# Where the weight conversions of a spectral-mixing and MLP kernel stand: behind the sums of batch 0's groups, and their late loads on GpSimd's queue

## The chip, the cores and the metric

The kernel runs on one core of a Trainium2 chip. A core has five engines with instruction queues of their own: TensorE (PE in the profile; its weight loads are the row PEld), VectorE (DVE), ScalarE (ACT), GpSimd (POOL) and SyncE (SP). Each engine works through its queue strictly in order, and waits on semaphores for the others. DMAs are issued from the queues of SP, ACT and POOL and run on 16 DMA engines that the three share. The metric is the device time of one execution in microseconds; a run gives one time, and the numbers compared are medians of several runs.

## The reference

Two blocks follow each other. The first filters each of 8 sequences of 3008 tokens with 256 channels in the frequency domain, the second is an MLP with the activation h - tanh(h):

```python
X = np.fft.rfft(x, axis=1)                       # x: (8, 3008, 256)
Y = X * (filt_r + 1j * filt_i)[None, :, :]
y = np.fft.irfft(Y, n=3008, axis=1).astype(np.float32)

h = y.reshape(24064, 256) @ w_in                 # (256, 2048), float64
g = h - np.tanh(h)
out = (g @ w_out).astype(np.float32)             # (2048, 256), float64
```

The two weight matrices arrive as 64-bit floats and are 512K numbers each.

## The kernel before, in words

**The transform.** 3008 is 64 x 47, so the transform is done in two matrix steps each way: over the 64 (`first`, matrices `f`), over the 47 (`forth`, matrices `mats`), the product with the filter (`filtered`), back over the 47 (`back`, `back0`) and back over the 64 (`last`, matrices `g`, product `pu`). The 32 rows between the two steps are worked in seven groups (`SLOTS`): six of 120 partitions and a last one of 48. Between the steps the data of the other batches pass through DRAM (`ct1`, `ct2`); for batch 0 the first step is turned on the chip instead (`first0` writes `turnt`, which lies in the space of `wd`; `across` transposes it), and only its way back goes through `ct2`.

**The weights.** [...] `converted` (L139) loads a piece of 128 x 512 raw numbers with one DMA (`raw`, L143, 512 KB) and makes 32-bit floats from the bits: one ACT step (L149) and six DVE steps (L151, L154, L157, L160, L162, L169; the pieces of the second matrix take L169 in two halves). It is a Python generator: each `next` issues one step. A quarter of a matrix is two such pieces ("jobs"); quarters 0 to 3 are the first matrix (`wu`), 4 to 7 the second (`wd`). `weights` (L210) strings jobs together and begins the load of a later job whenever one is done (`ahead`); `sums` (L194) then adds four products' worth of weight sums per quarter, which the steps of the second stage with seven products need.

**The order.** Nothing is scheduled by a tool: the order of each queue is the order in which the Python code issues (`tc.manual_schedule`). The code before the second stage (L934 to L1057) is batch 0's opening. It loads x in three pieces (L947 on SP, L952 on POOL), the half matrices `fh` on ACT's queue (L949), and the first three raw jobs on ACT's, SP's and POOL's queue (L945, L966). `warmer(n)` issues n products into a tile nobody reads. `first0(c)` works on the piece c of x; behind it `convert(7)` issues one job's steps. Then the loop over the seven groups (L1023) issues for group g: the filter rows of g+2 and `across(g+2)`, `forth` of g+1, then on DVE the sum and difference of group g (L292, L293, which read the product `pa` from PSUM) and the filter products (L303, L308, L309, L310); the sum L312 goes to POOL for all groups but the last; four conversion steps (L1040); and `back0` of g-1 on PE. In the iteration of group 5 it begins the late raw jobs on SP's queue (L1045) and the first loads of `first(2, ...)`: `f` (L242) and `x_sb` (L224, L230), three buffers each. Behind the loop come the products of batch 1's first piece (`first1`, L993), `back` of group 6 (L334), the load of `e` (L413) for the first `pu` and the rest of the early conversions.

The second stage runs steps U = 0, 1, 2, ...; four make one group of tokens. In step U it issues `up` for U, the activation (`shrink`) for U-1 and `down` for U-2. U < 4 use plain forms (`up_plain`, `down_plain`: two or four products of 448 columns, each PSUM bank copied by ACT or DVE, L542); from U = 4 on seven products replace eight (L469, L639), which need the sums of the weights. Quarter k of `wu` is needed at U = k, quarter k of `wd` at U = k + 2. Inside a step, hooks `d`, `e`, `s` and `t` place pieces of other work between the products: conversions (`converting`), the steps of the transforms of later batches (`steps`, `firsts`, `mids`) and the filter copies (`copies`, whose zero tile L1077 is set by POOL and written by SP, L1079).

```python
def e():
    next(dw, None)
    converting(1 + (U > 3))
```

## Time and profile before

| | |
|---|---|
| median of 3 runs | 2756.82 us (2756.11 to 2758.78) |
| the profiled execution | 2759.41 us, span 2757.4 us |
| mean granted clock of TensorE | 0.994 |
| busy share of the span | PE 98%, PEld 86%, ACT 63%, DVE 61%, POOL 47% |
| chain that ended last | PE 91%, DVE 5% |
| first product of group 0 across (L894) | 31.77 us |
| first product back of group 6 (L334) | 86.98 us |
| first `pu` product (L431) | 98.54 us |

A row of a timeline gives the start, the time, the engine, the line and the instruction with its tiles, the number of instructions merged into it, and in brackets how long the engine stood idle before it and what released it. "PE L872" is a matmul issued by line 872; rows of ACTq, SPq and POOL with DMA_DIRECT2D are DMA issues, not the transfers. A row of a source line gives the least, the median and the longest duration in nanoseconds. The granted clock is the share of full speed that the chip's throttle gave TensorE in a window.

### The profile page before, as it was taken

Reading aid. Unit: us, or ns where it says so; the run is one execution under the profiler, and the core shown is the slowest. Engines: PE = TensorE matmul, PEld = TensorE weight load, DVE = VectorE, ACT = ScalarE, POOL = GpSimd, SP = SyncE. Lnnn points to the kernel's source line nnn. Section 1 sums busy time; section 2 is a strip of 40 time slices with the busy share of each in tenths; the row PEclk is TensorE's granted clock in tenths of the full one; section 3 lists DMA queues with packets and bytes.
Section 4 is the critical chain, followed back from the end, with each engine's and each line's share of the span. In section 5 each row is a group of like instructions: output and inputs, shape, how many; then the busy total and the mean of one; then the engine's idle time right before and its main releaser. Section 6 shows DMA issues by size and latency. Waiting matters only on the chain.

```text
span 2757.4 us, 36442 instructions
## 1 busy us (share of the span) xinstructions
PE 2711.3 (98%) x12938; PEld 2367.4 (86%) x12938; DVE 1676.0 (61%) x2082; ACT 1732.1 (63%) x2595; POOL 1292.4 (47%) x1062
## 2 busy tenths in 40 slices
PE   8899999999999999999999999999999999999998
PEld 7578889888898888988889888898888988899887
DVE  6767766566556665666556665466655766644545
ACT  3466666666666666666666666666666666666665
POOL 3015445544554445544445455455444554455452
PEclk9899999999999999999999999999999999999999
DMA  7653322331233312433224232332322222111010
GB/s 203 212 169 88 85 63 71 88 98 49 64 75 102 89 48 60 106 76 79 53 65 109 66 80 53 94 78 67 84 51 69 53 63 53 30 26 32 22 25 17
DMA packets 337532, 207.77 MB, mean 75 GB/s; under 512 B 226390, under 2 KB 299042, under 8 KB 337085
## 3 DMA queue, kind: packets, MB, share of 16 engines
q1 hardware_dynamic: 296157, 151.08, 22.4%
q10 hardware_dynamic: 39056, 48.25, 5.8%
q0 software_dynamic: 2128, 6.03, 0.8%
q8 instruction: 104, 1.70, 0.3%
q14 instruction: 87, 0.71, 0.1%
HBM read 133.31 MB, written 74.97 MB: 76 GB/s over the span
## 4 chain that ended last, share of the span: by engine, by line
PE 91%; DVE 5%; issue 2%; DMA 1%; ACT 1%; ACTq 0%; SPq 0%; POOL 0%; DVEq 0%; POOLq 0%
PE o L639 38%; PE x L469 22%; PE z L469 11%; PE y L469 5%; PE pa L287 3%; PE pe L334 3%; PE pu L431 3%; PE pf L255 2%; PE o L693 1%; DVE h L591 1%; DVE h L525 1%; DVE h L492 1%; DVE xy L324 0%; PE pf L872 0%; PE o L539 0%
## 5 line engine op out<-in xcount | busy, mean ns | idle before, releaser
L639 PE MATMUL o<-t,wd 128*128 128x256 f32 (+1 forms) x3008 | 760.3, 375 | 0.0
L449 POOL TENSOR_TENSOR t<-h 128x512 f32<-128x512 f32 (+1 forms) x186 | 256.5, 1379 | 974.0 <-DVE h L591 856.9
L591 DVE TENSOR_TENSOR h<-h,y 128x1024 f32<-128x1024 f32 (+1 forms) x384 | 512.5, 1335 | 286.0 <-ACT y L587 285.5
L639 PEld LDWEIGHTS o<-t,wd 128*128 128x128 f32 x3008 | 570.5, 190 | 69.5 <-issue 2.4
L469 PE MATMUL x<-tu,wu 128*128 128x256 f32 (+1 forms) x2256 | 574.2, 377 | 1.3 <-ACT u L475 1.0
L639 PE MATMUL o<-h,wd 128*128 128x256 f32 (+1 forms) x2256 | 571.0, 376 | 1.8 <-DVE h L591 1.8
L469 PEld LDWEIGHTS x<-tu,wu 128*128 128x128 f32 x2256 | 421.7, 190 | 62.1 <-ACT u L475 9.2
L639 PEld LDWEIGHTS o<-h,wd 128*128 128x128 f32 x2256 | 424.2, 190 | 52.7 <-DVE h L591 2.6
L475 ACT COPY s<-x 128x512 f32<-128x512 f32 (+1 forms) x188 | 108.7, 578 | 502.2 <-PE x L469 489.7
L581 ACT ACTIVATE y<-h 128x1024 f32<-128x1024 f32 (+1 forms) x384 | 400.1, 1042 | 13.8 <-ACT a L256 6.4
L584 ACT ACTIVATE y<-y 128x1024 f32<-128x1024 f32 (+1 forms) x384 | 399.1, 1039 | 12.1
L587 ACT ACTIVATE y<-y 128x1024 f32<-128x1024 f32 (+1 forms) x384 | 399.8, 1041 | 5.4 <-ACT a L256 0.8
L509 DVE TENSOR_TENSOR h<-z,u 128x512 f32<-128x512 f32 (+1 forms) x188 | 127.6, 679 | 259.1 <-ACT u L475 258.0
L475 ACT COPY u<-x 128x512 f32<-128x512 f32 (+1 forms) x376 | 215.0, 572 | 86.5 <-PE x L469 64.9
L451 POOL TENSOR_TENSOR t<-h 128x512 f32<-128x512 f32 (+1 forms) x186 | 266.8, 1434 | 0.0
L450 POOL TENSOR_TENSOR t<-h,t 128x512 f32<-128x512 f32 (+1 forms) x186 | 259.8, 1397 | 14.6
L452 POOL TENSOR_TENSOR t<-h,t 128x512 f32<-128x512 f32 (+1 forms) x186 | 263.3, 1416 | 0.0
L517 DVE COPY h<-x 128x512 f32<-128x512 f32 (+1 forms) x188 | 127.9, 680 | 157.3 <-PE x L469 156.7
L469 PE MATMUL z<-ut,wu 128*128 128x256 f32 (+1 forms) x752 | 190.3, 375 | 0.0
L469 PE MATMUL z<-tu,wu 128*128 128x256 f32 (+1 forms) x752 | 190.1, 375 | 0.0
L469 PE MATMUL x<-ut,wu 128*128 128x256 f32 (+1 forms) x752 | 190.1, 375 | 0.0
L469 PE MATMUL y<-ut,wu 128*128 128x256 f32 (+1 forms) x752 | 190.0, 375 | 0.0
(143 smaller groups left out, 3096.2 us busy)
## 6 DMA issues: line engine op xcount, KB each, us to landing
e<-ct SPq DMA_DIRECT2D x48, 512.0 KB
ct<-e ACTq DMA_DIRECT2D x96, 240.0 KB
ct<-a ACTq DMA_DIRECT2D x82, 256.0 KB
a<-ct SPq DMA_DIRECT2D x42, 480.0 KB
ft<-filt SPq DMA_DIRECT2D x42, 480.0 KB
out_dram<-ot SPq DMA_DIRECT2D x1248, 16.0 KB
x_sb<-in_x_dram SPq DMA_DIRECT2D x154, 128.0 KB
gt<-g SPq DMA_DIRECT2D x48, 256.0 KB
```

The costliest lines, as they stand in the source:

```text
L449: by.tensor_sub(t[0], b[0][1], b[0][0])
L450: by.tensor_sub(t[1], b[1][1], t[0])
L451: by.tensor_sub(t[2], b[1][1], b[0][1])
L452: by.tensor_sub(t[3], b[1][0], t[1])
L469: nc.tensor.matmul(bank[:, k], wu[:, q - 1, (2 * u + k) * 128:(2 * u + k + 1) * 128], rhs[q - 1], start=(first and k == 0), stop=True, ski ...
L475: ACT.copy(t, X)
L517: V.tensor_copy(h[:, 2, :, 0:w], X)
L581: ACT.activation(y[k], ht[k], AF.Arctan, scale=TURN)
L584: ACT.activation(y[k], y[k], AF.Tanh, scale=BEND)
L587: ACT.activation(y[k], y[k], AF.Square, scale=SCALE, accum_out=y_sums[:, 2 * U + k // 2:2 * U + k // 2 + 1])
L591: V.tensor_mul(ht[k], ht[k], y[k])
L639: nc.tensor.matmul(product(q), wd[:, q - 1, (2 * u + k) * 128: (2 * u + k + 1) * 128], rhs[q - 1][:, k], start=(u == 0 and k == 0 and q == ...
```

## The change

The change is made in the opening and in the hooks of the second stage; the functions that compute are untouched.

- Quarter 3 of the first matrix leaves the early jobs: `early` converts quarters 0 to 2 (six jobs for eight). The late jobs are quarters 4, 3, 5, 6, 7 in this order, ten for eight, and their sums move back by two jobs.
- Raw job 0 is loaded on ACT's queue behind all three `fh` (the first matrix of the transform), where it stood behind the second.
- The warm-up products: 17, 2 and 3 for 13, 5 and 8 in the opening; 4 new ones ahead of `back` of group 6 and 8 for 10 behind it.
- Four conversion steps are issued behind `across(0)`, ahead of group 0. In groups 1 to 5 three steps stand between the sum and difference (L292, L293) and the filter products, where four stood behind these in groups 0 to 5. Three more follow the loop. The rest of the early jobs comes behind the issue of `e`'s load, and four steps of the late jobs are issued before the second stage's tiles are opened, four in place of sixteen behind that.
- The late raw jobs are issued from POOL's queue in place of SP's.
- In the second stage, `e` issues one step up to U = 2 and three from U = 3 on (one up to U = 3, two from U = 4 on); `t` always issues two (one up to U = 1).

```diff
@@ -931,7 +931,7 @@
             f0 = pro.tile([128, NH, 128], F32, name="f0")
             warm_b = cst.tile([128, 1], F32, name="warm_b")
             V.memset(warm_b, 0.0)
-            jobs = parts_of(range(4))
+            jobs = parts_of(range(3))
             sgn = cst.tile([128, 1], F32, name="sgn")
             for half in range(2):
                 V.memset(sgn[64 * half:64 * half + 64], 1.0 - 2 * half)
@@ -942,8 +942,7 @@
                 xt = big([128, 8, DM], F32, "x0")
                 xs.append(xt)
                 if c == 2:
-                    began += [begun(tiles0, job, queue=q)
-                              for job, q in zip(jobs, (ACT, nc.sync))]
+                    began.append(begun(tiles0, jobs[1], queue=nc.sync))
                 nc.sync.dma_start(xt[0:64], dram(x.tensor, r * DM, [[NR * DM, 64], [1, 8 * DM]]))
                 fh = pro.tile([128, 8, 64], F32, tag="e1", bufs=5, name="fh")
                 ACT.dma_start(fh, half_d[:, 64 * r:64 * r + 512])
@@ -956,6 +955,7 @@
                     n = cols.stop - cols.start
                     V.tensor_scalar(out=f0[:, r:r + 8, to:to + n], in0=fh[:, :, cols],
                                     scalar1=sgn, scalar2=None, op0=ALU.mult)
+            began.insert(0, begun(tiles0, jobs[0], queue=ACT))
             nc.sync.dma_start(one, one_d)
             nc.sync.dma_start(mats[:, 0:3 * KM], mats_d[:, 0:3 * KM])
             ACT.activation(warm_b, warm_b, AF.Arctan)
@@ -969,7 +969,7 @@
             fts[1] = filters_of(1)
             turned_rows()
 
-            early = weights(tiles0, range(4), G, began, 3)
+            early = weights(tiles0, range(3), G, began, 3)
             next(early)
 
             def convert(n):
@@ -977,12 +977,12 @@
                 for _ in range(n):
                     next(early, None)
 
-            warmer(13, filt[2][:, 0])
+            warmer(17, filt[2][:, 0])
             first0(0)
-            warmer(5)
+            warmer(2)
             convert(7)
             first0(1)
-            warmer(8)
+            warmer(3)
             convert(7)
             first0(2)
             def first1(x1):
@@ -1000,6 +1000,7 @@
                     yield
 
             a2 = {0: across(0)}
+            convert(4)
             last_g = len(SLOTS) - 1
             summed = (last_g,)
 
@@ -1029,6 +1030,8 @@
                 if g < last_g:
                     there[g + 1] = there0(g + 1)
                 next(there[g][0])
+                if 0 < g < last_g:
+                    convert(3)
                 xy = there.pop(g)[1]
                 chain = filtered(g, xy, fts.pop(g), V, V if g in summed else G, pro)
                 nn = next(chain)
@@ -1036,25 +1039,28 @@
                     next(chain)
                 if g in summed:
                     next(chain)
-                if g < last_g:
-                    convert(4)
                 ended.append((back, (0, g, xy, z0)) if g in summed else (back0, (g, nn)))
                 if g:
                     way_back()
                 if g == last_g - 1:
-                    late = weights(tiles1, (4, 5, 6, 7), nc.sync, [],
-                                   after={3: (0,), 5: (1,), 7: (2, 3, 4, 5, 6)})
+                    late = weights(tiles1, (4, 3, 5, 6, 7), G, [],
+                                   after={5: (0,), 7: (1,), 9: (2, 3, 4, 5, 6)})
                     next(late)
                     fs = first(2, z1, [(1, c) for c in range(4, NX)])
                     next(fs)
+            convert(3)
             for _ in range(2):
                 next(ones_1)
+            warmer(4)
             way_back()
             e2s[0] = load_e2(*groups[0])
+            convert(100)
+            next(late)
             for _ in ones_1:
-                convert(5)
-            warmer(10)
-            convert(100)
+                pass
+            for _ in range(3):
+                next(late)
+            warmer(8)
 
         with tc.tile_pool(name="dn", bufs=2) as dn, \
                 tc.tile_pool(name="ps", bufs=1, space=bass.MemoryType.PSUM) as ps:
@@ -1092,7 +1098,7 @@
             total = 4 * len(groups)
             for _ in last(0, z1):
                 pass
-            for _ in range(16):
+            for _ in range(4):
                 next(late)
             def planned(p):
 
@@ -1146,7 +1152,7 @@
                 def e():
 
                     next(dw, None)
-                    converting(1 + (U > 3))
+                    converting(3 if U > 2 else 1)
 
                 def s():
 
@@ -1172,7 +1178,7 @@
                             gens[b] = what(b, z1)
                             next(gens[b])
                         next(gens[b])
-                    converting(1 + (U > 1))
+                    converting(2)
                     if k and U > 1:
                         next(copies, None)
 
```

## The prediction, made before the result was known

> **What bounds the kernel now.** I read the page first (busy shares, chain), then the stages of the first 180 us, then the timelines of PE, DVE, ACT, POOL and SP there, then the waits. Lines L... are those of the kernel before; U counts the 256-wide steps of the second stage from 0.

> ```profile
> PE 2711.3 (98%) x12938; PEld 2367.4 (86%) x12938; DVE 1676.0 (61%) x2082; ACT 1732.1 (63%) x2595; POOL 1292.4 (47%) x1062
> 60.00:80.00 20.00, 15.46 (x58) 10.68 (x56) 19.47 (x26) 5.61 (x10) 5.14 (x5) 0.83 0.94 282
> 360.00:2700.00 2340.00, 2325.85 (x11222) 2056.82 (x11221) 1393.40 (x1673) 1504.70 (x2247) 1163.44 (x945) 1.00 0.26 66
> ```

> Columns of a stage: window, length, busy us of PE, PEld, DVE, ACT, POOL, then granted clock, DMA share, GB/s. From 360 us on PE is busy all but 14 of 2340 us: whatever moves the start of that stream, or a gap in its beginning, moves the end one for one. In the groups of batch 0 it is DVE that is full (19.47 of 20 us). So the change is priced in two places: when the first `pu` product of the second stage starts (98.54 us), and what PE loses just behind it.

> ```profile
> 12.84 5.24 PE L872 MATMUL pf<-f,x 128*128 128x128 f32 x30 [2.88 <-DMA x<-in_x_dram]
> 27.11 3.73 PE L872 MATMUL pf<-f,x 128*128 128x128 f32 x32
> 31.77 1.06 PE L894 MATMUL pq<-one_sb,wd 128*120 128x128 f32 x8 [0.93 <-ACT wd L875]
> 33.62 1.99 PE L287 MATMUL pa<-a,mats_sb 120*120 120x256 f32 x8 [0.78 <-DVE a L898]
> 79.96 0.69 PE L920 MATMUL pe<-nn,mats_sb 120*120 120x256 f32 x2 [1.35 <-POOL nn L312]
> 83.08 1.89 PE L993 MATMUL pf<-x,f 128*128 128x256 f32 x8
> 86.98 2.36 PE L334 MATMUL pe<-xy,mats_sb 48*48 48x256 f32 x8 [2.01 <-DVE xy L314]
> 92.84 5.60 PE L882 MATMUL warm<-f 128*128 128x256 f32 x20
> 98.54 1.97 PE L431 MATMUL pu<-gt,e 128*128 128x128 f32 x16
> 116.88 2.04 PE L255 MATMUL pf<-x_sb,f 128*128 128x256 f32 x4 [3.98 <-DMA x_sb<-in_x_dram]
> ```

> PE waits for DVE's last group (2.01 us, L314), goes back (L334) and fills with warm-up products until 98.44. Behind that it stands 3.98 us for `x_sb`.

> **Part 1, the opening** (raw job 0 behind the third `fh` on ACT's queue; warm-ups 13, 5, 8 become 17, 2, 3).

> ```profile
> 18.76 0.66 ACT L149 ACTIVATE top<-raw 128x512 f32<-128x512 f32 x1
> 21.17 3.48 ACT L875 COPY wd<-pf 128x512 f32<-128x512 f32 x4 [1.75 <-PE pf L872]
> q10 hardware_dynamic: 704, 1.31, 16.9%
> 22.15 0.43 DVE L954 COPY f<-fh 128x512 f32<-128x512 f32 x1 [13.73 <-DMA fh<-f_half]
> 30.17 1.50 DVE L875 COPY wd<-pf 128x512 f32<-128x512 f32 x2
> 22.60 0.57 POOL L968 DMA_DIRECT2D mats_sb<-mats  x1 [0.98 <-DMA x<-in_x_dram]
> L154 DVE TENSOR_SCALAR top<-top x8: 422/427/1373, 23.7 to 96.5; 128x512 int32<-128x512 int32 x8
> L162 DVE SCALAR_TENSOR_TENSOR low<-raw,low x8: 684/692/1634, 25.4 to 98.1; 128x512 f32<-128x512 uint32 x8
> ```

> ACT's queue (q10, 0 to 30 us) moves 1.31 MB, three `fh` and one raw job, and its last piece lands at 22.15. Swapped, `fh` comes early and raw job 0 is that last piece: same bytes, so about 22.1 us. ACT is in order: its first L149, at 18.76 until now, waits until then and holds the four copies behind it (3.48 us); the second L149 follows near 26.1 and ends at 26.8. Then DVE's second conversion, three instructions of 0.43 and three of 0.69 (3.4 us), until 30.2, and its two L875 copies (1.50): 31.7, as before. So nothing is gained there, though PE, with `x` landed at 22.6 and a full clock, is done with L872 near 26.3. It thus stands 5.4 us where it stood 0.93. What that does, the clock shows:

> ```profile
> 9.75:13.16 3.41, 0.53 (x4) 0.34 (x4) 0.00 (x0) 0.00 (x0) 0.00 (x0) 1.00 1.05 265
> 13.16:16.57 3.41, 3.41 (x19) 3.41 (x18) 0.00 (x0) 1.42 (x2) 0.00 (x0) 0.50 1.04 264
> 115.50:119.00 3.50, 2.12 (x5) 1.79 (x6) 1.58 (x4) 0.56 (x2) 0.00 (x0) 0.51 0.96 281
> 119.00:122.40 3.40, 3.40 (x6) 1.67 (x6) 0.45 (x1) 1.59 (x3) 0.00 (x0) 0.50 0.73 188
> ```

> After 2.88 us without work the next 3.41 us run at half clock; after 3.98 us it is 6.9 us. So L894 and L287 of group 0 (0.9 and 1.9 us on the path) run at half clock: 0 to +2.8 us. I take +2.1, nearer the upper end since this idle is longer than either row's. [...]

> **Part 2, the groups** (L1040's 4 steps behind the products become 3 steps between L293 and L303 in groups 1 to 5; 4 steps stand ahead of group 0).

> ```profile
> 35.71 0.69 DVE L292 TENSOR_TENSOR xy<-pa,xy 120x512 f32<-120x512 f32 x1 [2.15 <-PE pa L287]
> 39.82 0.69 DVE L310 TENSOR_TENSOR xy<-xy,filt 120x512 f32<-120x512 f32 x1
> 40.88 1.37 DVE L154 TENSOR_SCALAR top<-top 128x512 int32<-128x512 int32 x1
> 86.15 0.68 DVE L314 TENSOR_TENSOR xy<-nn 48x512 f32<-48x512 f32 x1
> 40.66 1.31 POOL L312 TENSOR_TENSOR nn<-nn,xy 120x512 f32<-120x512 f32 x1 [7.74 <-DVE xy L310]
> 78.35 1.55 POOL L312 TENSOR_TENSOR nn<-nn,xy 120x512 f32<-120x512 f32 x1 [6.55 <-DVE xy L310]
> L509 DVE TENSOR_TENSOR h<-z,u x184: 586/692/693, 181.7 to 2691.8; 128x512 f32<-128x512 f32 x156, 128x448 f32<-128x448 f32 x28
> L591 DVE TENSOR_TENSOR h<-h,y x384: 1081/1217/2359, 114.2 to 2738.6; 128x1024 f32<-128x1024 f32 x160, 128x896 f32<-128x896 f32 x32
> ```

> (a) Fewer steps. By the order of instructions DVE has 20 conversion instructions between L292 of group 0 and L314; 13 stay. The three put ahead of group 0 (0.43, 0.43, 0.69) fall into the 2.15 us wait, ACT's L149 ahead of them into ACT's wait for the same product. The seven gone are four of 0.43 and three of 0.69: -3.8 us.

> (b) The collision. After each L310 POOL runs L312, and the DVE conversion beside it takes 0.94 us more (L154 1.37 for 0.43; L162 at most 1.63 for 0.69). Six times, -5.8 us with the last one's 1.07, if the DVE instruction that comes there now does not collide. That is L292 of the next group, with one operand in PSUM. The nearest row with such operands is L509: never above 0.693, with POOL at 47%, while L591, with both in SBUF, spreads up to 2.36. So I take it as free; the other end is no gain at all.

> (c) L314 ends at 86.83 + 2.1 - 3.8 - 5.8 = 79.3. But then PE is late next. From L312 of group 5 it needs 83.08 - 79.96 = 3.1, then half of L993 (1.9) and the 4 new warm-ups (8 instructions like L993's, 1.9) before L334. L310 of group 5 ends 6.2 us ahead of L314's end (4.8 as from 35.71 to 40.51, and two of 0.68), L312 1.6 later: 74.7, and 6.9 make 81.6. PE's wait for that L312 grows from 1.35 toward the 2.88 that halved the clock; a half window costs 1.7, I add half of it: L334 at 82.4 instead of 86.98.

> (d) From there to the first `pu`:

> ```profile
> 91.94 0.34 SPq L413 DMA_DIRECT2D e<-ct  x1
> L431 PEldq EVENT_SEMAPHORE  x2: 51/1098/2146, 96.2 to 96.3; - x2
> ```

> The store of `ct`, the load of `e` behind it (91.94), then `pu`. The weight load passed its first wait at 96.25 and stood 2.1 us in its second. If the first is for `e`, `e` lands 9.3 us behind L334's start; if the second is, 11.4. PE itself needs only 2.3 + 1.9 + 3.6 = 7.8 (8 warm-ups in place of 10). I take 9.3, as the warm-ups ended at 98.44 and explain the second: `pu` at 91.7, -6.8; with 11.4, -4.7.

> **Part 3, the late weights** (raw jobs from POOL's queue, quarter 3 of the first matrix among them).

> ```profile
> SPq L143 <- DVE conv L162: 14.0, 3, 10.5
> 104.63 0.38 SPq L143 DMA_DIRECT2D raw<-in_moe_w_out_dram  x1
> 109.61 0.63 SPq L230 DMA_DIRECT2D x_sb<-in_x_dram  x1
> L143 POOL DMA_DIRECT2D raw<-in_moe_w_in_dram x6: 724/730/767, 17.4 to 79.9; - x6
> 137.50:152.00 14.50, 14.50 (x55) 8.87 (x54) 9.08 (x21) 9.34 (x15) 0.00 (x0) 1.00 0.34 103
> ```

> SP stood 10.5 us at a raw load until 104.63, as its buffer was not yet converted; `e` of group 1, `f` and `x_sb` were queued behind. The `x_sb` issued at 109.61 is PE's 3.98 us gap, and the half clock to 122.4 costs 2.75 more (half of 5.5). In the new order SP has no raw load, and the third `f`/`x_sb` set needs no buffer to come free: it follows `e`, two `ct` stores and group 1's loads, a few us of issue. Bounds 0 and -6.7; I take -6.0, as later sets still wait for the product three before them and share the DMA with raw loads.

> POOL issues ten late raw loads of 0.73 (7.3 us) for SP's eight of 0.39. Behind them in POOL's queue stand only the memset of zeros and, through it, SP's zeroing of `filt` with the `x_sb` loads after it; POOL is idle there (0.00 in the last row). I put +0.2; the upper bound is the old gap, 6.7.

> DVE gets 22 steps later than before (14 of quarter 3's two jobs, 8 of the others), at about 0.55 each 12 us, in U=0 to U=4. The last row is about U=3: DVE is busy 9.08 of 14.5 us, and gets 8 more steps (4.4 us) there, 13.5. Bounds 0 (all in idle time) to +12 (all on PE's path); blocks of 3 steps (1.7 us) stand ahead of copies that free PSUM, so +2.6.

> Sum: -6.8 - 6.0 + 0.2 + 2.6 = -10.0. The profiled execution took 2759.41 (span 2757.4 and 2.0 around it), 2.6 above the median of the runs, 2756.82. So 2749.4 on its scale, and 2747 on the median's.

> **Rivals.**
> A. The clock takes the start's gain: half clock over two windows (6.9 us, 3.4 lost) from L920 to L334 of the last groups and again at `pu`, where PE waits some 1.5 us for `e`. For it: fewer warm-ups, and 2.88 us sufficed. Against: the 1.35 us at 79.96 cost nothing. +6.8 for the 0.8: 2753.
> B. Part 2's order does not do what it seems to: L292 collides with L312 too and (b) is 0. L312 of group 5 ends near 80.5, L334 comes at 88.2, `pu` at 97.5, only -1.0: 2752.6. Against: L509.
> C. The gap comes back elsewhere: SP waits for the zeros behind POOL's raw loads, or a later `x_sb` is late: +6.0, 2753. For it: three buffers only. Against: POOL is idle.
> D. Slower: DVE becomes the bound from U=2 to U=5. All 22 steps land on PE's path, 12 us, and two waits over 2.88 us halve the clock, 3.4 each: 18.8 for the 2.6, net +6: 2763. It decides once DVE overruns PE's 14.5 us a U by some 4 us in four of them. Against: 13.5 above.
> E. Raw loads of POOL land late; L149 then holds ACT and its PSUM copies. Each hold like SP's gap, 6.7: one gives 2753.5, three 2767. No row speaks for it: the issues stay within 0.724 to 0.767 with DVE 97% busy. [...]

> **How the numbers follow.** About 0.2% (5.5 us) is what a measurement of this kernel can tell from no change. Forecast 0.49 (its own range 2740 to 2751, faster); A 0.13, B 0.07, C 0.10 (each near -4: two thirds same, one third faster); D 0.14, slower; E 0.05, 0.03 of it slower; 0.02 slower for what is not named. Faster 0.59, same 0.22, slower 0.19. Below, the range takes the bounds -6.8, -6.7 and 0 with the part of group 0's +2.1 and 0.8 that may not come: 2740. Above it takes A to C and 4 us more of DVE's steps: 2758. D and the rest of E stay out.

> **What would show it.** Right: no DVE conversion above 1 us in the groups; L334 near 82 and `pu` near 92; no `x_sb` gap and clock 1.00 from 100 us on. Wrong: `pq` of group 0 far from 31.7; half clock between 75 and 95; PE waiting for DVE or ACT between 125 and 185 us.

## The result, and the profile after

The changed kernel takes 2751.78 us (median of 20 runs, 2749.70 to 2753.41) against 2757.45 us of the kernel before (20 runs, 2754.96 to 2762.54). The ratio is 0.9978, with a 95% interval of 0.9971 to 0.9985: faster by 5.7 us, a little over half of the 10.0 us forecast. The profiled execution took 2753.31 us (span 2751.4), 1.5 above its median; that of before lay 2.0 above. Between the two profiled executions 6.0 us of span are gone. One execution of the last variant below took 10293 us and is left out of that variant's median.

Four stages of the changed kernel (columns as in the prediction: window, length, busy us of PE, PEld, DVE, ACT, POOL, granted clock, DMA share, GB/s):

```profile
83.00:88.00 5.00, 5.00 (x23) 3.57 (x23) 4.07 (x8) 2.78 (x6) 0.00 (x0) 1.00 1.00 374
...
92.60:99.40 6.80, 4.75 (x18) 4.25 (x19) 0.00 (x0) 1.06 (x2) 0.00 (x0) 0.52 0.98 343
...
137.50:152.00 14.50, 14.50 (x55) 9.56 (x54) 12.38 (x27) 8.66 (x16) 0.00 (x0) 1.00 0.60 190
360.00:2700.00 2340.00, 2326.08 (x11223) 2060.11 (x11222) 1390.59 (x1672) 1504.23 (x2248) 1159.13 (x943) 1.00 0.26 66
```

The long stretch from 360 us on is what it was. The difference is made before it, and the timeline of the changed kernel there shows where (start, time, engine, line, idle time before it):

```profile
32.00 1.94 PE L894 MATMUL pq<-one_sb,wd 128*120 128x128 f32 x8 [4.79 <-issue]
38.54 0.69 DVE L292 TENSOR_TENSOR xy<-pa,xy 120x512 f32<-120x512 f32 x1 [2.35 <-PE pa L287]
...
52.23 0.43 DVE L151 TENSOR_SCALAR top<-top 128x512 f32<-128x512 f32 x1 [1.24 <-ACT top L149]
...
74.53 0.66 PE L918 MATMUL pe<-nn,mats_sb 120*120 120x256 f32 x2 [0.87 <-DVE nn L309]
75.15 1.26 POOL L312 TENSOR_TENSOR nn<-nn,xy 120x512 f32<-120x512 f32 x1 [4.83 <-DVE xy L310]
76.36 1.45 POOL L143 DMA_DIRECT2D raw<-in_moe_w_out_dram  x2
76.46 0.69 PE L920 MATMUL pe<-nn,mats_sb 120*120 120x256 f32 x2 [1.27 <-POOL nn L312]
77.77 1.41 POOL L143 DMA_DIRECT2D raw<-in_moe_w_in_dram  x2
80.33 0.68 DVE L314 TENSOR_TENSOR xy<-nn 48x512 f32<-48x512 f32 x1
83.13 1.93 PE L334 MATMUL pe<-xy,mats_sb 48*48 48x256 f32 x8
85.83 0.45 ACTq L338 DMA_DIRECT2D ct<-e  x1
90.14 0.34 SPq L413 DMA_DIRECT2D e<-ct  x1
94.65 3.65 PE L431 MATMUL pu<-gt,e 128*128 128x128 f32 x16 [4.21 <-DMA e<-ct]
100.44 1.67 PE L539 MATMUL z<-ut,wu 128*128 128x448 f32 x4
115.17 1.13 PE L255 MATMUL pf<-x_sb,f 128*128 128x256 f32 x4 [1.45 <-ACT a L256]
118.71 1.67 PE L693 MATMUL o<-h,wd 128*128 128x448 f32 x4
```

Three rows of the kernel before give the same places there:

```profile
89.98 0.34 ACTq L338 DMA_DIRECT2D ct<-e  x1
...
101.99 1.67 PE L539 MATMUL z<-ut,wu 128*128 128x448 f32 x4
...
125.28 1.67 PE L693 MATMUL o<-h,wd 128*128 128x448 f32 x4
```

Group 0 starts 2.8 us later than before (38.54 for 35.71). L334 comes 3.85 us earlier (83.13 for 86.98), and so does `pu` (3.9, 94.65 for 98.54), but the sixteen `pu` products run at half clock (3.65 us for 1.97, granted clock 0.52 in that window), and of the gain 1.55 us are left at the second product of U = 0 (100.44 for 101.99). The 3.98 us for `x_sb` are gone, a wait of 1.45 us for ACT's copy L256 stands in that place, and at the first L693 the lead is 6.57 us. It ends at 6.0.

Two readings are to be told apart. Either e's lateness is the price of the raw loads, which POOL now issues at 76 to 79 us, behind L312 of group 5, where SP issued them at 67 to 71: they share the DMA with the last stores of `ct` (374 GB/s from 83 to 88 us), and L413 has to wait for those stores. Or it is something else: the order of the stores on ACT's queue, the later start of group 0, or the clock.

### The profile page after: what moved, and what is told of

Its sections match the earlier page's. It is cut to its first block, busy times and chain, and to the rows that moved or that the text cites. A ratio compares the mean times of both kernels' runs of the same rounds, so it can differ in the third digit from the quotient of the medians.

```text
span 2751.4 us, 36435 instructions
## 1 busy us (share of the span) xinstructions
PE 2706.0 (98%) x12934; PEld 2366.6 (86%) x12934; DVE 1669.0 (61%) x2082; ACT 1730.6 (63%) x2595; POOL 1296.8 (47%) x1070
## 4 chain that ended last, share of the span: by engine, by line
PE 90%; DVE 4%; DMA 2%; issue 2%; ACT 2%; ACTq 0%; POOL 0%; SPq 0%; DVEq 0%; POOLq 0%
PE o L639 38%; PE x L469 22%; PE z L469 11%; PE y L469 5%; PE pa L287 3%; PE pu L431 3%; PE pe L334 3%; PE pf L255 2%; DMA raw<-in_moe_w_in_dram 1%; PE o L693 1%; DVE h L591 1%; DVE h L525 1%; DVE h L492 1%; DMA ct<-e 0%; DVE xy L324 0%
## 5 line engine op out<-in xcount | busy, mean ns | idle before, releaser
L591 DVE TENSOR_TENSOR h<-h,y 128x1024 f32<-128x1024 f32 (+1 forms) x384 | 512.2, 1334 | 286.6 <-ACT y L587 286.0
L475 ACT COPY s<-x 128x512 f32<-128x512 f32 (+1 forms) x188 | 108.6, 578 | 501.4 <-PE x L469 486.5
L509 DVE TENSOR_TENSOR h<-z,u 128x512 f32<-128x512 f32 (+1 forms) x188 | 127.6, 678 | 258.4 <-ACT u L475 257.3
L475 ACT COPY u<-x 128x512 f32<-128x512 f32 (+1 forms) x376 | 214.7, 571 | 86.3 <-PE x L469 65.1
```

The source lines that it names most:

```text
L475: ACT.copy(t, X)
L591: V.tensor_mul(ht[k], ht[k], y[k])
```

## The experiments

All ratios are to the kernel before, with 95% intervals; its median was 2756.7 to 2757.7 us beside each of them. Single executions of one kernel lie up to 8 us apart, so a difference of 2 us between two variants is read from the trace, and the medians only say whether they contradict it.

**The queue alone, in the kernel before.**

```diff
-late = weights(tiles1, (4, 5, 6, 7), nc.sync, [],
+late = weights(tiles1, (4, 5, 6, 7), G, [],
```

> The kernel before with one word changed: the late raw jobs go by POOL's queue (part 3's queue alone). Theory: the x_sb gap and its half clock are gone (-5 to -6.7), but the raw loads start behind L312 of group 5, near 80 us, and delay the ct stores and e: pu 2 to 3 us later than 98.54 and with half clock, +2 to +5; net -1 to -4, about 2755. Rival, raw loads do not delay e: the whole gap is gained, 2751. Rival, the queue made no difference: 2757.4.

2757.57 us, ratio 1.0001 (0.9992 to 1.0010): nothing. Its timeline:

```profile
81.53 2.91 POOL L143 DMA_DIRECT2D raw<-in_moe_w_out_dram  x4
88.83 1.92 PE L334 MATMUL pe<-xy,mats_sb 48*48 48x256 f32 x8
...
118.66 1.13 PE L255 MATMUL pf<-x_sb,f 128*128 128x256 f32 x4 [1.03 <-ACT a L256]
```

The gap for `x_sb` is gone, as forecast. But L334 comes 1.85 us later than in the kernel before, `pu` at 99.31, two waits for L256 appear (1.03 and 0.86 us), and at U = 4 one for ACT's L475 (1.21 us). Of the 1.85 us, 0.96 were there at group 0 already (L292 at 36.67 for 35.71), ahead of anything that the edit touches, and at 83 to 88 us the clock was 0.60. L413 follows the last store by 2.83 us for 1.96 in the kernel before. In this execution the queue thus gains 4.5 us from the second product of U = 0 to the first L693 (18.8 us for 23.3), but PE comes there 2.4 us late, and a lead of 1.0 us is left at the end; the medians show none. The 6.0 us forecast for this part aren't a gain that the queue makes by itself.

**The queue undone, in the changed kernel.**

```diff
-late = weights(tiles1, (4, 3, 5, 6, 7), G, [],
+late = weights(tiles1, (4, 3, 5, 6, 7), nc.sync, [],
```

> The changed kernel with the late raw loads back on SP's queue (part 3's queue alone undone). Theory: they are then issued near 69 us and done before the last ct stores, so e is issued by 88 and pu starts by 92.5 (2 us earlier), but SP stands behind a raw load again, x_sb is late, and PE stands some 4 us with half clock behind it: 5 to 6.7 us lost, net 2 to 4 us slower than the changed kernel, 2754 to 2756. Rival, raw loads have no part in the late e: pu again near 94.7 and the gap on top, 2757 to 2758. Rival, the gap was not due to SP's wait: no gap, 2750.

2751.65 us, ratio 0.9980 (0.9971 to 0.9989), the same as the changed kernel. The timeline shows one loss traded for another:

```profile
83.12 1.93 PE L334 MATMUL pe<-xy,mats_sb 48*48 48x256 f32 x8
...
85.82 0.34 ACTq L338 DMA_DIRECT2D ct<-e  x1
87.79 0.33 SPq L413 DMA_DIRECT2D e<-ct  x1
...
92.33 1.97 PE L431 MATMUL pu<-gt,e 128*128 128x128 f32 x16 [1.91 <-DMA e<-ct]
...
111.56 1.31 PE L255 MATMUL pf<-x_sb,f 128*128 128x256 f32 x4 [2.51 <-DMA x_sb<-in_x_dram]
```

Its stages, columns as above:

```profile
83.00:88.00 5.00, 5.00 (x23) 3.57 (x23) 4.24 (x8) 2.80 (x5) 0.53 (x1) 1.00 0.67 218
...
110.00:116.00 6.00, 4.43 (x10) 2.63 (x11) 2.85 (x5) 2.75 (x6) 0.00 (x0) 0.72 0.99 307
```

From L918 at 74.5 us to the last store the rows of the two kernels are the same within 0.02 us, and so this pair tells the most. With the raw loads issued at 68 to 71 the DMA moves 218 GB/s for 374 from 83 to 88 us, L413 follows the last store by 1.97 us for 4.31, and `pu` starts 9.2 us behind L334 for 11.5. Behind that SP is held at the raw loads again (they take it from 90.77 to 100.36, 8.7 us of which are one wait for DVE's L162), and `x_sb` costs 2.51 us and the clock (0.72).

**The opening undone.**

```diff
-began.append(begun(tiles0, jobs[1], queue=nc.sync))
+began += [begun(tiles0, job, queue=q) for job, q in zip(jobs, (ACT, nc.sync))]
...
-began.insert(0, begun(tiles0, jobs[0], queue=ACT))
...
-            warmer(17, filt[2][:, 0])
+            warmer(13, filt[2][:, 0])
...
-            warmer(2)
+            warmer(5)
...
-            warmer(3)
+            warmer(8)
```

> The changed kernel with the opening as before: raw job 0 between the second and third fh, warm-ups 13, 5 and 8. Theory: the new opening only cost, as raw job 0 landed last and PE stood 4.8 us and ran at half clock: L894 of group 0 stays near 31.8 but at full clock, L292 of group 0 comes at 35.7 in place of 38.5, and all that follows up to pu 2.8 us earlier: 2749.0. Rival, the gain is lost again at e, which waits for DMAs: pu 0 to 1 us earlier, 2751 to 2752. Rival, the new opening helped in another way: slower than the changed kernel.

2750.80 us, ratio 0.9975 (0.9966 to 0.9985); not told apart from the changed kernel.

```profile
32.67 1.30 PE L894 MATMUL pq<-one_sb,wd 128*120 128x128 f32 x8 [1.98 <-issue]
34.75 3.77 PE L287 MATMUL pa<-a,mats_sb 120*120 120x256 f32 x8 [0.78 <-DVE a L898]
38.63 0.69 DVE L292 TENSOR_TENSOR xy<-pa,xy 120x512 f32<-120x512 f32 x1 [2.41 <-PE pa L287]
```

Here DVE had the third `fh` at 23.10 (22.15 in the kernel before), PE stood 1.98 us ahead of `pq`, and L287 still fell to half clock (3.77 us for 1.99). Group 0's first sum is at 38.63, no earlier than with the new opening. With the same opening the kernel before and the variant with the queue alone had a pause of 0.93 us and no half clock there, and the last variant below one of 3.10 us and the half clock (granted clock 0.58 from 31 to 34 us). So this run doesn't price the opening; it shows that a pause of 2 us at this place can be enough for the half clock.

**More warm-up products.** Ten more behind L334; in a second variant four more there and two ahead of group 5's way back.

```diff
-            warmer(8)
+            warmer(18)
```

> The changed kernel with 18 instead of 8 warm-up products behind the way back of group 6, so that PE works until e lands. If the half clock that followed PE's 4.21 us of idle time cost path time: the first pu starts at 94.7 as in the changed kernel, takes 1.97 us in place of 3.65, the granted clock stays 1.00 from 92 to 100, and the end comes 2.2 us earlier, 2749.6 on the medians. If the slow window was hidden: the same time as the changed kernel, 2751.8. If the warm-ups themselves are in the way: pu later than 94.7.

```diff
+                if g == last_g:
+                    warmer(2)
                 if g:
                     way_back()
...
-            warmer(8)
+            warmer(12)
```

> Changed kernel, with 12 warm-up products for 8 behind back of group 6 and two more ahead of group 5's way back; nothing else moved. Theory 'clock': in the profiles so far the windows at half clock at 74 to 83 us (four of eight variants) and at the first pu (four of eight) come from idle time of PE just before; with PE busy to about 92.3 and in the gap at 74 to 76, L334 starts at 83 to 84 in every execution, the sixteen pu products take 2.0 us in place of 3.65 and the products behind them run at full speed, 2.9 us less: 2749 us. Rival 'paid out later': as with ten more warm-ups, the conversions and ACT's order in U = 1 to 3 give the gain back, 2751.8 or more.

2753.24 us, ratio 0.9983 (0.9974 to 0.9992), and 2752.14 us, ratio 0.9981 (0.9972 to 0.9990). In both the sixteen `pu` products run at full clock; the first variant's products themselves held `pu` until 95.75. The second:

```profile
82.26 1.93 PE L334 MATMUL pe<-xy,mats_sb 48*48 48x256 f32 x8
92.88 1.97 PE L431 MATMUL pu<-gt,e 128*128 128x128 f32 x16 [1.59 <-DMA e<-ct]
...
154.04 1.13 PE L469 MATMUL x<-tu,wu 128*128 128x256 f32 x4 [1.52 <-ACT u L475]
```

Its profiled execution is 2.9 us of span shorter than the changed kernel's, the number of the clock theory, but not by its sum: at the second product of U = 0 it leads by 4.1 us (96.33 for 100.44), 1.8 of them by an earlier `pu`. And it is the fastest of its eleven (2750.43), the changed kernel's is among the slowest of its twenty, and the medians show no gain. A part of the lead is paid back at U = 4, where the first wait for L475 is 1.52 us (0.29 in the changed kernel). The half clock at `pu` costs 2.3 us in the execution that has it, and the typical execution isn't explained by it. The expectation fell.

**What holds `e`: the stores' order or the raw loads.** In one variant the raw loads behind quarter 4's two begin only once `e` has landed; in the other the first four stores of L998 go to SP's queue, so that L338's stand behind none of them.

```diff
-late = weights(tiles1, (4, 3, 5, 6, 7), G, [], ...)
-next(late)
+two = [begun(tiles1, job, G) for job in parts_of((4,))]
...
 e2s[0] = load_e2(*groups[0])
+gate_e = cst.tile([1, 1], F32, name="gate_e")
+G.tensor_copy(gate_e, e2s[0][0][0:1, 0, 0:1])
+late = weights(tiles1, (4, 3, 5, 6, 7), G, two, ...)
+next(late)
```

> Changed kernel, only the two raw loads of quarter 4 are begun in group 5; all other late raw loads are issued by POOL only once e has landed (a small POOL copy of e stands ahead of them). Theory 'raw traffic': the 2 MB of raw loads that POOL issues at 76 to 79 us slow the stores of batch 0's way back and e itself, so that e's load is issued at 90.1 and pu starts at 94.65; here e is issued near 88 and pu starts near 92.3 at full clock, as with SP's queue, and the time is 2.3 us below the changed kernel (2749.5). Rival 'order of the stores': the stores wait behind those of batch 1's first piece on ACT's queue; then pu stays near 94.6 and the time is that of the changed kernel (2751.8). Rival 'later conversions bound': pu is earlier, but the conversions of quarter 3 start late, ACT stands in L149 for raw, and the gain is lost by U = 4 (2752 or more).

```diff
-                    (ACT if r < 4 else nc.sync).dma_start(
+                    nc.sync.dma_start(
```

> Changed kernel, with the first four stores of batch 1's first piece (L998) on SP's queue, so that the last stores of batch 0's way back (L338) stand behind no other transfer on ACT's. Theory 'order of the stores': e is issued about 1.5 us earlier (88.6), pu starts near 93.1, time 2750.3. Rival 'raw traffic': the bytes are the same, e stays at 90.1 and pu at 94.6 within 0.5 us, time 2751.8.

The first: 2750.14 us, ratio 0.9975 (0.9964 to 0.9985). L413 follows the last store by 2.03 us, and `pu` follows L334 by 9.34:

```profile
84.55 1.92 PE L334 MATMUL pe<-xy,mats_sb 48*48 48x256 f32 x8
...
87.25 0.34 ACTq L338 DMA_DIRECT2D ct<-e  x1
89.28 0.34 SPq L413 DMA_DIRECT2D e<-ct  x1
...
93.89 1.97 PE L431 MATMUL pu<-gt,e 128*128 128x128 f32 x16 [2.04 <-DMA e<-ct]
```

L334 itself came 1.4 us later there than in the changed kernel, after a stretch at half clock between 74 and 83 us (granted clock 0.81), which is why `pu` isn't at 92.3. The second: 2753.35 us, ratio 0.9985 (0.9976 to 0.9994); L413 at 90.06, 3.3 behind the last store, `pu` at 94.55. The variants with more warm-up products, whose stores stand in the old order, have the same 3.3 (twelve, 84.96 to 88.27) and 2.6 (eighteen, 86.73 to 89.33), so nothing of it is shown to be the order's, and it brought no time. Two different edits, issuing the raw loads earlier or all but two of them later, bring the distance from the last store to L413 back to 2.0 us: their traffic is the cause. Over all the variants the distance is 1.9 to 2.5 us in the six that keep raw loads out of the stores' way and 2.6 to 4.3 in the seven profiles, the changed kernel's among them, in which POOL issues four ahead of the stores.

**The place of the conversion steps in the groups.**

```diff
-                if 0 < g < last_g:
-                    convert(3)
                 xy = there.pop(g)[1]
...
+                if 0 < g < last_g:
+                    convert(3)
                 ended.append(...)
```

> Changed kernel, with the three conversion steps of groups 1 to 5 back behind the filter products, as before the change. Theory (b) of the prediction: L157, L162 and L169 run beside POOL's L312 again and show up to 1.6 us; group 6's L314 ends 3 to 5 us later than 81.0, L334 starts near 86 to 87 against 83.1, pu near 97 to 98, and the time rises by 3 us to about 2754.8. Rival 'the place does not matter, only the number of steps': L314 ends near 81 and the time stays 2751.8. Rival 'e binds': L334 is later, but the loads of e have drained in the meantime and pu moves by under 1 us.

2752.88 us, ratio 0.9987 (0.9978 to 0.9996). The collisions are back:

```profile
37.96 0.69 DVE L292 TENSOR_TENSOR xy<-pa,xy 120x512 f32<-120x512 f32 x1 [2.41 <-PE pa L287]
47.82 1.64 DVE L162 SCALAR_TENSOR_TENSOR low<-raw,low 128x512 f32<-128x512 uint32 x1
...
77.35 1.63 DVE L157 SCALAR_TENSOR_TENSOR top<-raw,top 128x512 int32<-128x512 int32 x1
...
84.79 0.68 DVE L314 TENSOR_TENSOR xy<-nn 48x512 f32<-48x512 f32 x1
85.62 1.90 PE L334 MATMUL pe<-xy,mats_sb 48*48 48x256 f32 x8 [0.40 <-DVE xy L314]
96.11 1.97 PE L431 MATMUL pu<-gt,e 128*128 128x128 f32 x16 [3.21 <-DMA e<-ct]
```

With L154 at 55.20 and L160 at 61.85 four instructions take 0.95 us more than alone, and from L292 to L314 DVE needs 46.8 us for 41.8. Of these 5.0 us 3.8 are the four collisions; 1.0 is a longer wait for ACT's L149 (2.24 us at 71.91, for 1.24 in the changed kernel), which isn't shown to be due to the place. L334 is only 2.5 us later, since products that PE had to fill with anyway stood in between, and `pu` 1.5 us, since more of the raw loads had landed by then (L413 at 91.6, 3.3 behind the last store for 4.3). So 5 us on DVE are 1.5 at `pu`. The profiled execution doesn't even show these, as its `pu` runs at full clock; the ratios differ by about 2.5 us with overlapping intervals, between the theory's 3 and nothing.

**Combinations.** The first four late raw loads by SP, the six later ones by POOL; the same with the warm-up products of above; and that with the copies L256 of batch 1's later pieces on DVE (eight of them; the expectation says four).

```diff
-late = weights(tiles1, (4, 3, 5, 6, 7), G, [],
+late = weights(tiles1, (4, 3, 5, 6, 7), G,
+               [begun(tiles1, job, nc.sync) for job in parts_of((4, 3))],
```

> Changed kernel, with the first four late raw loads (quarters 4 and 3) on SP's queue as before the change and only the six later ones on POOL's. Theory: the early four are issued at 68 to 71 in place of 76 to 79 and are out of the way of e, pu starts near 92.3 at full clock (as with all on SP's queue), and SP is not held by a raw load, so that the wait for x_sb near 111 stays away; the time is 2.3 us below the changed kernel, 2749.5. Rival 'ACT's order binds behind it': at U = 1 PE waits for the copies of L256 behind ACT's activations, whatever the start; the gain is given back there and the time is that of the changed kernel, 2751.8.

> The kernel before this one with the first four late raw loads on SP's queue as well. Theory: the terms add: e is issued 2 us behind the last store (about 87.8) in place of 4.3, pu starts near 92.5 at full clock and the raw loads leave the wait for x_sb alone: 2751.8 - 2.1 - 2.9 = 2746.8 us. Rival 'paid out later': pu is at 92.5, but the waits for ACT at U = 1 and U = 4 grow, 2749 us.

```diff
-            ACT.copy(a1, pf)
-            ACT.dma_start(dram(ct1[b], ...), a1)
+            (V.tensor_copy if b == 1 else ACT.copy)(a1, pf)
+            (nc.sync if b == 1 else ACT).dma_start(dram(ct1[b], ...), a1)
```

> The kernel before this one, with the four copies L256 of batch 1's later pieces on DVE for ACT, and their stores on SP's queue. Theory 'ACT's order binds in U = 1': the wait of 1.45 us for L256 at 114 us and the 0.4 us ahead of it go, 1.5 us below the kernel before this one: 2745.3 us. Rival 'DVE binds as well': the four copies of 0.69 us push the conversions, and PE waits as long for DVE or, at U = 4, for ACT's L475; no gain, 2746.8 us or slower.

The split: 2748.97 us, ratio 0.9970 (0.9959 to 0.9981). With the warm-up products: 2750.25 us, ratio 0.9972 (0.9961 to 0.9983). With the copies on DVE: 2753.15 us, ratio 0.9981 (0.9972 to 0.9990). The split's profiled execution:

```profile
85.58 1.93 PE L334 MATMUL pe<-xy,mats_sb 48*48 48x256 f32 x8
...
88.29 0.34 ACTq L338 DMA_DIRECT2D ct<-e  x1
90.20 0.33 SPq L413 DMA_DIRECT2D e<-ct  x1
...
94.69 2.62 PE L431 MATMUL pu<-gt,e 128*128 128x128 f32 x16 [1.81 <-DMA e<-ct]
...
114.46 1.13 PE L255 MATMUL pf<-x_sb,f 128*128 128x256 f32 x4 [1.46 <-ACT a L256]
```

Both theories' numbers are there: L413 1.91 us behind the last store, `pu` 9.1 behind L334, no gap for `x_sb`. L334 was 2.5 us later than in the changed kernel, by a half clock from 74 to 83 us (0.62), and this execution (2752.23) is the slowest of its seven, which begin at 2747.01. With the warm-up products L334 stands at 82.87 and `pu` at 92.58 at full clock (1.00 from 92 to 100 us), and the seven executions lie within 1.5 us of each other, but not lower: the terms don't add.

The wait for L256 stays in all of them. With the copies on DVE it became a wait of 2.63 us for DVE and the clock fell behind it (0.83 from 110 to 120 us, L255 2.05 us for 1.13):

```profile
114.33 2.05 PE L255 MATMUL pf<-x_sb,f 128*128 128x256 f32 x4 [2.63 <-DVE a L256]
```

So the theory that ACT's order alone binds in U = 1 fell: from 108 to 116 us DVE was busy 6.96 and ACT 6.76 of 8 us there, and the wait moved from one to the other. The last run joined the split and the old opening:

> Changed kernel, with the first four late raw loads on SP's queue and the opening as before the change. Theory: the two gains add: about 1 us for the opening and 2 us for the early raw loads, ratio to the kernel before 0.9967 (2748 us against 2757), L334 at 83 to 84, e issued 2 us behind the last store. Rival 'the clock's windows decide': the opening brings nothing by itself (group 0's first sum stands at 38.6 in both), only other windows fall to half clock; the ratio is that of the early raw loads alone, 0.9970 to 0.9978.

2748.82 us (seven executions), ratio 0.9970 (0.9959 to 0.9981): L334 at 83.11, `pu` at 92.92 with half clock (3.59 us for 1.97), group 0's first sum at 38.5. The ratio can't tell the theory's 0.9967 from the rival's 0.9970; the trace speaks for the rival, as group 0 starts no earlier with the old opening. The best versions, the split with and without the old opening, are 8 to 8.5 us faster than the kernel before, and their intervals overlap with the changed kernel's.

## Why the prediction was right, and by which steps too much

The sign, the whole range (2740 to 2758) and the two places were right. The forecast's own range ended at 2751, 0.8 us below the result, and by the number alone rivals A, B and C, put at 2752.6 to 2753, are nearer than the 2747 of the sum. The traces decide: B is excluded by L292, C by the missing gap, and A came in part. The size was 4 us too large, and the terms show where:

| term | forecast, us | profile | what it was |
|---|---|---|---|
| start of `pu` (part 2) | -6.8 | -3.9 | 98.54 to 94.65 |
| clock at `pu` | 0 (rival A) | +2.3 | -1.55 left at the product at 100.44 |
| `x_sb` (part 3) | -6.0 | -5.0 | -1.55 to -6.57 at the first L693 |
| POOL's queue and DVE's later steps | +2.8 | +0.6 | -6.57 to -6.0 at the end |
| sum | -10.0 | -6.0 | |

- **Part 1 held.** `pq` came at 32.0 (31.7 forecast), PE stood 4.79 us (5.4), the clock fell (0.57 from 31 to 34 us), and L292 of group 0 came 2.8 us later (2.1, upper end 2.8).
- **Part 2 (a) and (b) held.** From L292 of group 0 to L314 DVE needed 50.4 us before and needs 41.8, 8.6 less for the 9.6 forecast. No conversion in the groups takes above 0.7 us, and L292 beside L312 0.69 at most: the six collisions of (b), 5.8 us, are gone, and 13 conversion instructions stand there for 20, as (a) counted. The 1.0 us that are missing go into a wait of 1.24 us for ACT's L149 (52.23 us), which the prediction didn't have. With the steps back behind the products it is 46.8, with four collisions, 3.8 us. L292, which reads its other input from PSUM, took 0.61 to 0.69 us while POOL ran L312; that the PSUM operand is the reason was the prediction's reading of L509 and L591 (0.69 and 2.36 us at most in the kernel before), and no run tests it apart.
- **(c) was near.** L312 of group 5 ended at 76.4 us for 74.7, and PE needed 6.7 us from there (6.9): L334 at 83.1 for 82.4, without the half clock that had been put in for a part.
- **(d) failed.** "`e` lands 9.3 us behind L334's start" was read from the kernel before, whose raw loads were out of the way by then. Part 3 had counted what the loads cost on POOL's queue, not that POOL reaches them 8 us later than SP (76.4 for 68.6 with SP's queue), behind L312, and that their bytes then meet the last stores. It is 11.5 us; with the loads issued early, or behind `e`, it is 9.1 to 9.8 in six variants. That the other end of the range, 11.4, is nearly the same number is chance: it had been set aside as the warm-up products' wait.
- **Part 3's gap went, but not for nothing.** `x_sb` is no longer waited for; a wait of 1.45 us for ACT's copies came in its place, more than the 1.0 us that are missing. In the kernel before the queue alone gained 4.5 us at this place, with two waits for ACT in the gap's stead, and lost most of it elsewhere: 0.9 us more between the last store and L413, half clock ahead of L334 (0.60 from 83 to 88 us) and at `pu` (0.58 from 100 to 104), a later opening that the edit doesn't touch, and U = 4. How much of this is typical isn't shown; its median is that of the kernel before.
- **DVE's later steps cost less.** From 137.5 to 152 us DVE is busy 12.4 us (13.5 forecast) and PE stands nowhere; from 125 to 185 us DVE is busy 48.6 us for 39.0, and PE waits 1.07 us for 0.82; +0.6 in all for +2.8. Rival D is excluded, and so is E: from 60 us on ACT nowhere waits for a raw load at L149.
- **Rival A came half.** The half clock at `pu` is there in the profiled execution; at L920 it isn't, though it is in four of the variants. What it takes from the median stays open: variants that keep the clock up at both places have the same medians.
- **The signs.** Of the signs of being right, `pu` near 92 failed (94.65); the others came, with a clock of 1.00 from 100 to 125 us. Of the signs of being wrong two came in small: half clock from 92.9 us on, and PE waiting for ACT's L475 (0.29 and 0.78 us at 157 and 160 us, where the kernel before has one wait of 0.82).

## What to carry to other kernels

A load that is moved to another queue is issued when that queue's engine comes to it (here at 76.4 us on POOL's queue for 68.6 on SP's), so its bytes move in time as well: look at what is stored or loaded in the new place before counting the wait it removes. When a wait at the head of a full stage goes, ask which engine ended next there; here ACT's copies stood 1.45 us behind the gap of 3.98. And where one profiled execution differs from its neighbours by a window of the clock, take the price of that window from the trace, and let the medians say whether it is typical.

## What the runs showed of the hardware that was not expected

```profile
72.37:75.78 3.41, 1.95 (x8) 1.03 (x7) 3.31 (x6) 0.77 (x2) 0.63 (x1) 1.00 0.88 259
75.78:79.19 3.41, 2.73 (x13) 2.34 (x14) 3.31 (x5) 0.58 (x1) 3.40 (x5) 1.00 0.61 175
...
73.33:76.74 3.41, 1.66 (x7) 1.15 (x8) 3.34 (x5) 0.23 (x1) 2.31 (x3) 1.00 0.47 134
76.74:80.16 3.42, 3.42 (x10) 2.56 (x9) 3.28 (x6) 0.59 (x1) 1.72 (x3) 0.50 0.93 298
```

In the one a window's end cuts the second pause; in the other a single window holds 1.8 us of the 2.15, with PE busy for 1.66, and the next runs at half clock. Up to 125 us the 14 profiles have 25 windows at full clock in which PE is busy for under 1.45 us, and the half clock follows all of them; it follows 7 of 12 with 1.45 to 1.8 us, 1 of 48 with 1.8 to 2.6, and none of 333 with more. In the kernel before and the changed kernel alone these are 5 of 5, 0 of 1, 1 of 9 and 0 of 45. At `pu` a pause of 2.51 us was followed by the half clock (last variant, 3.59 us for 1.97): it lay in one window, PE busy for 0.93 us. One of 3.21 us, in the variant with the steps behind the products, was cut by a window's end at 94.78 us and wasn't. In the variant with L998's stores on SP's queue pauses that add up to 2.15 us, neither of them over 1.3, were enough.
